# A recurrent-memory attention kernel: products of 128 weight columns made as two products of 64 side by side

## The chip, the cores and the metric

The kernel runs on one core of one Trainium2 chip. The metric is the device time of one execution in microseconds (us); lower is better. A profile is one execution taken by the hardware profiler; its span goes from the first to the last instruction.

## What is computed

Two layers of attention with a recurrent memory (A), each followed by a dense block (B), over 2048 tokens of width 512, in bf16. Attention goes by segments of 32 tokens; ahead of each segment stand 8 memory rows, which are the first 8 output rows of the segment before it, so that segments of one layer must follow one another. There are 32 heads of 128.

```python
for s in range(n_seg):                                   # 64 segments
    h = concatenate([mem, xs], axis=1)                   # 8 + 32 = 40 rows
    q, k, v = h @ Wq, h @ Wk, h @ Wv                     # 32 heads of 128
    scores = where(mask, q @ k.T * scale, -1e9)
    o = (softmax(scores) @ v) @ Wo
    mem = o[:, :M]; outs.append(o[:, M:])

x = x + A(layernorm(x)); x = x + B(layernorm(x))         # B: relu(x @ w1) @ w2, inner width 1376
x = x + A(layernorm(x)); x = x + B(layernorm(x))         # the same weights again
```

## The kernel before

All weights stay in SBUF. The work is a chain of 68 steps, written out one after the other. Step k does segment k of the first layer (act 0) and segment k - 4 of the second layer (act 1), as far as both exist: steps 4 to 63 are the 60 two-layer steps (`single` is false), the four before and the four after have one layer. The two segments of a two-layer step lie side by side in the tile `HT` (512 features in four chunks c4, by 2 x 40 rows), so that one product with the query or key weights has 80 moving columns; in a one-layer step it has 40.

In a step, in this order on TensorE:

- `qk(0, ...)`: queries and keys of heads 0 to 15, in batches of 6, 6 and 4 heads (`qk_batch`). Each head takes four accumulating products of 128 x 128 weights (`lhsT` = `W_sb`, `rhs` = `HT`), 128 products in all, into PSUM tiles `qp` of a pool of three banks. ScalarE casts the queries to `QT` (L597), VectorE the keys to `KT` (L599).
- `block`: some products of the output projection of the step before (`wox`, L373: 64 weight columns, 256 moving columns, in the left and the right half of the array's columns in turn, named by `tile_position`), in some steps also value products (`vp`, L310).
- `scores` (L625): 32 products of 40 weight columns, again left and right in turn.
- `qk(1, ...)`: queries and keys of heads 16 to 31, another 128 products. While they run, VectorE and ScalarE make the exponentials of the first half.
- `dense_h` (L522): the first dense product of segment k - 2, 11 x 4 = 44 products of 128 x 128 weights with up to 64 moving columns; ScalarE applies the relu. In the steps with value products it is cut in two parts, with other work between.
- scores of the second half, more of `block`, the second dense product (`dense_y`, L543, 64 weight columns), the transposes of the second half's probabilities (`transpose_p`, L675, 64 weight columns), the weighted values (L701), the output of the memory rows (L633), values of the next step (L354), the new memory (L857) and its values (L797).

The order on TensorE, VectorE, GpSimd and the DMA-issuing SyncE is the order written in the program (`manual_schedule` names these four); on ScalarE the order is a planner's. `tc.high_priority` marks the chain of the recurrence for that planner.

A product in the program is two instructions on TensorE, a weight load (PEld in the profile) and the product proper (PE).

Of the kernel before, what the change touches and what calls it, by code (L numbers as in the profile page):

```python
# [22 lines left out]
def kernel(  # L23
# [14 lines left out]
    nc = tc.nc  # L38
    _, S, Dm = A_x.shape
    _, H, Dh = A_Wq.shape[0], A_Wq.shape[1], A_Wq.shape[2]  # L40
# [4 lines left out]
    L = M + SEG  # L45
# [4 lines left out]
    NC4 = Dm // 128  # L50
# [45 lines left out]
    def span(d):  # L96
        offs = ([0] if has0(d) else []) + [o for o, _ in slots_of.get(d, [])]
        return base(d) + min(offs), base(d) + max(offs) + 32
# [52 lines left out]
    w1_sb = const.tile([128, NC4, Dff], BF)  # L151
# [35 lines left out]
    HT = const.tile([128, NC4, 2, L], BF)  # L187
# [95 lines left out]
    def layers(k):  # L283
        return [a for a in range(2) if (has0, has1)[a](k)]
# [216 lines left out]

    def dense_h(d, parts=slice(None), behind_exp=False):
        if not 0 <= d <= LAST:
            return
        lo, hi = span(d)
        n = hi - lo

        def cols(c4):  # L510
            return xnT_tiles[d + 2][:, c4, lo:hi]

        if not parts.start:
            hT_tiles[d] = wk.tile([128, NFC, 64], BF, tag="hT", bufs=1, name="hT")
        hT = hT_tiles[d]
        pieces = ((8, NFC), (0, 4), (4, 8)) if d == LAST - 1 else ((8, NFC), (0, 8))
        for f0, f1 in pieces[parts]:
            hp = ps_fill.tile([128, 8, 64], F32, tag="fill", name="hp")
            for fc in range(f0, f1):
                u = F_LAST + 128 * fc if fc < NFC - 1 else 0  # L520
                for c4 in range(NC4):
                    nc.tensor.matmul(hp[:, fc - f0, 0:n], lhsT=w1_sb[:, c4, u:u + 128],  # L522
                                     rhs=cols(c4), start=(c4 == 0), stop=(c4 == NC4 - 1))
            if (f0, f1) == (4, 8):
                nc.vector.tensor_scalar_max(out=hT[:, f0:f1, 0:n], in0=hp[:, 0:f1 - f0, 0:n], scalar1=0.0)
            elif behind_exp:
                with tc.issue_after(last_exp[0].ins):
                    nc.scalar.activation(out=hT[:, f0:f1, 0:n], in_=hp[:, 0:f1 - f0, 0:n], func=ACTF.Relu)
            else:
                nc.scalar.activation(out=hT[:, f0:f1, 0:n], in_=hp[:, 0:f1 - f0, 0:n], func=ACTF.Relu)  # L530
# [51 lines left out]
    def qk_batch(n, h0, nh, a_lo, a_hi, between=None):  # L582
        ncol = (a_hi - a_lo) * L
        res = {}

        for W_sb, nm in (((Wq_sb, "QT"), (Wk_sb, "KT")) if n < 2 else ((Wk_sb, "KT"), (Wq_sb, "QT"))):
            qp = ps_c.tile([128, HB, 2 * L], F32, tag="c")
            for hi in range(nh):
                h = h0 + hi
                for c4 in range(NC4):  # L590
                    nc.tensor.matmul(qp[:, hi, 0:ncol], lhsT=W_sb[:, c4, h * Dh:(h + 1) * Dh],  # L591
                                     rhs=HT[:, c4, a_lo:a_hi, :], start=(c4 == 0), stop=(c4 == NC4 - 1))
            dst = wk.tile([128, nh, 2 * L], BF, tag=f"{nm}{n}", bufs=1, name=nm)
            if nm == "QT":
                if between:
                    between()
                nc.scalar.copy(out=dst[:, 0:nh, a_lo * L:a_hi * L], in_=qp[:, 0:nh, 0:ncol])  # L597
            else:
                nc.vector.tensor_copy(out=dst[:, 0:nh, a_lo * L:a_hi * L], in_=qp[:, 0:nh, 0:ncol])  # L599
            res[nm] = dst  # L600
        return res["QT"], res["KT"]
# [3 lines left out]
    def qk(hf, act, between=None, behind=None):  # L605
        res = []
        for n, (o, nh) in enumerate(BATCHES):
            res.append((o, nh) + qk_batch(n, 16 * hf + o, nh, act[0], act[-1] + 1, None if n else between))
            if n == 0 and behind:
                behind()  # L610
            if hf and n > 0 and (n == 2 or len(act) == 1):
                masks(*act[n - 1:n])
        return res
# [319 lines left out]
    def step(k):  # L933
# [54 lines left out]
        if single:  # L988
            block(k, part, mid)
        elif light:  # L990
            dense_h(k - 2, slice(0, 1))
            block(k, part, 16)
        else:
            dense_h(k - 2)
# [3 lines left out]
        if single:  # L998
            dense_h(k - 2, slice(0, 1) if k == LAST else slice(None))
            block(k, mid, H)  # L1000
            if k == LAST:
                keep_busy(3)
        elif light:
            dense_h(k - 2, slice(1, None), True)
            block(k, 16, H)
        else:
            if not single:
                evict_behind.append(last_exp[0].ins)
            block(k, part, H)
            evict_behind.clear()  # L1010
# [56 lines left out]
    with tc.manual_schedule(engines={mybir.EngineType.PE, mybir.EngineType.DVE, mybir.EngineType.SP,  # L1067
# [23 lines left out]
        d = LAST - 1  # L1091
# [10 lines left out]
        for fc in order:  # L1102
            fs = 128 if fc < NFC - 1 else F_LAST
            for q in range(4):
                u, j = divmod(q, 2)
                nc.tensor.matmul(sp_banks[0][32 * q:32 * q + 32, 0:256], lhsT=hT_tiles[d][0:fs, fc, SEG * u:SEG * u + SEG],  # L1106
                                 rhs=w2_flat[0:fs, fc * Dm + 256 * j:fc * Dm + 256 * j + 256],
                                 start=(fc == order[0]), stop=(fc == order[-1]), tile_position=(0, 32 * q))
# [42 lines left out]
```

## Time and profile before

| | us |
|---|---|
| median of 3 runs | 1582.98 |
| lowest, highest | 1580.97, 1584.96 |
| span of the profiled execution | 1580.0 |
| TensorE busy (PE) | 1548.6, 98% |
| weight loads (PEld) | 1286.3, 81% |
| VectorE busy | 1277.3, 81% |
| ScalarE busy | 734.7, 47% |
| GpSimd busy | 349.8, 22% |

Of the profiled execution the page gives the span alone; it lies 1.0 us under the fastest run and 3.0 under the median, which is what stands before the first and behind the last instruction and the spread between runs. Busy times of TensorE contain the tail of the last product of a group, so products are better compared by the distance from one start to the next.

### The profile page before, as it was taken

To read this page: it belongs to the slowest core of one execution; us is meant where nothing else is said; L and a number is where in the kernel's file an instruction comes from. 1 tells how busy PE (TensorE), PEld (TensorE's weight loads), DVE (VectorE), ACT (ScalarE), POOL (GpSimd) and SP (SyncE) were. 2 spreads that over 40 slices of the span, in tenths; PEclk is the share of its full clock that TensorE was granted. 3 is DMA by queue.
4 is the path that set the end of the run, shared out by engine and by line. 5 is a ranking of instruction groups with operands and counts; after the bars stand their busy time and mean duration, and the time that the engine had idled before them with its cause. 6 is when DMAs were issued, how large, how long until landed. Compare 5 with 4: busy or idle time off the path is not lost. (4 is left out here: it accounts for less than half of the span.)

```text
span 1580.0 us, 95139 instructions
## 1 busy us (share of the span) xinstructions
PE 1548.6 (98%) x42866; PEld 1286.3 (81%) x42866; DVE 1277.3 (81%) x3300; ACT 734.7 (47%) x1762; POOL 349.8 (22%) x670
## 2 busy tenths in 40 slices
PE   5899999999999999999999999999999999999998
PEld 3677888888888888888888888988888898888876
DVE  3578888888888888888888888888888888887866
ACT  3435445454544545454454545445454544545433
POOL 2012122222222222222122222212222221222110
PEclk9999999999999999999999999999999999999999
DMA  9734432434353244434433343443443344333331
GB/s 369 246 77 76 87 84 78 81 92 79 78 92 84 78 82 94 80 76 91 84 80 80 99 80 76 88 84 79 77 99 77 72 87 80 82 74 95 75 69 41
DMA packets 222021, 146.26 MB, mean 93 GB/s; under 512 B 123464, under 2 KB 215984, under 8 KB 221616
## 3 DMA queue, kind: packets, MB, share of 16 engines
q1 hardware_dynamic: 218448, 135.96, 38.8%
q8 instruction: 336, 5.51, 1.5%
q0 software_dynamic: 3072, 4.20, 1.1%
q14 instruction: 69, 0.57, 0.1%
q10 hardware_dynamic: 96, 0.03, 0.0%
HBM read 65.41 MB, written 45.35 MB: 70 GB/s over the span
## 5 line engine op out<-in xcount | busy, mean ns | idle before, releaser
L597 ACT CAST QT<-qp 128x480 bf16<-128x480 f32 (+3 forms) x408 | 201.5, 494 | 433.4 <-PE qp L591 433.1
L591 PE MATMUL qp<-HT,Wq_sb 128*128 128x80 bf16 (+1 forms) x8704 | 371.3, 200 | 3.2 <-POOL HT L786 1.2
L591 PEld LDWEIGHTS <-Wq_sb 128*128 128x128 bf16 x8704 | 325.9, 100 | 35.2 <-issue 27.5
L591 PE MATMUL qp<-HT,Wk_sb 128*128 128x80 bf16 (+1 forms) x8704 | 347.3, 199 | 1.7 <-issue 1.3
L591 PEld LDWEIGHTS <-Wk_sb 128*128 128x128 bf16 x8704 | 319.5, 100 | 2.6 <-issue 1.6
L664 POOL TENSOR_TENSOR P_sb<-es,sm 128x320 bf16<-128x320 f32 x185 | 130.8, 721 | 714.8 <-ACT QT L597 299.4
L599 DVE CAST KT<-qp 128x480 bf16<-128x480 f32 (+3 forms) x408 | 220.3, 565 | 36.3 <-PE qp L591 32.9
L643 DVE TENSOR_REDUCE mx<-sp 128x8 f32<-128x320 f32 x256 | 115.1, 487 | 133.1 <-PE sp L625 130.9
L373 PE MATMUL wox<-Wo_sb,OTx 128*64 128x256 bf16 x2880 | 173.6, 273 | 0.0
L373 PEld LDWEIGHTS <-OTx 128*64 128x64 bf16 x2880 | 150.2, 110 | 2.9
L649 ACT ACTIVATE es<-es 128x320 f32<-128x320 f32 x256 | 109.5, 468 | 61.9 <-DVE es L647 61.0
L797 PE MATMUL vm<-Wv_sb,HTm 128*32 128x512 bf16 x2176 | 129.4, 379 | 1.8 <-DVE KT L599 1.0
L354 PE MATMUL v<-Wv_sb,xnT 128*32 128x512 bf16 x2048 | 128.8, 378 | 0.0
L633 PE MATMUL wo<-Wo_sb,OTm 128*32 128x512 bf16 x2144 | 128.6, 380 | 0.0
L659 DVE TENSOR_REDUCE sm<-es 128x8 f32<-128x320 f32 x256 | 117.4, 459 | 13.5 <-ACT es L649 5.0
L617 DVE CAST sp<-maskb 128x320 f32<-128x320 bf16 x256 | 118.3, 483 | 0.0
L647 DVE TENSOR_TENSOR es<-sp,mx 128x320 f32<-128x320 f32 x256 | 113.6, 482 | 1.5
L543 PE MATMUL sp<-w_sb,hT 128*64 128x256 bf16 (+4 forms) x1452 | 103.9, 276 | 0.4 <-issue 0.4
L522 PE MATMUL hp<-xnT,w_sb 128*128 128x64 bf16 (+1 forms) x2948 | 98.5, 192 | 0.9 <-issue 0.5
L801 ACT CAST VmS<-vm 128x512 bf16<-128x512 f32 x134 | 78.5, 586 | 44.4 <-PE vm L797 42.5
L222 POOL TENSOR_TENSOR mv<-mv,mhalf_t 128x1 f32<-128x1 f32 x82 | 45.8, 558 | 224.6 <-DVE mv L221 218.9
L797 PEld LDWEIGHTS <-HTm 128*32 128x32 bf16 x2176 | 54.7, 97 | 48.8 <-issue 3.1
(125 smaller groups left out, 2088.5 us busy)
## 6 DMA issues: line engine op xcount, KB each, us to landing
Vs<-vd SPq DMA_DIRECT2D x96, 256.0 KB
vd<-vst SPq DMA_DIRECT2D x181, 128.0 KB
vmd<-VmS SPq DMA_DIRECT2D x134, 128.0 KB
Vs<-vmd SPq DMA_DIRECT2D x254, 32.0 KB
Vs<-vmd SPq DMA_DIRECT2D x60, 128.0 KB
Wq_sb<-in_A_Wq_dram SPq DMA_DIRECT2D x2, 2048.0 KB
Wk_sb<-in_A_Wk_dram SPq DMA_DIRECT2D x2, 2048.0 KB
Wv_sb<-in_A_Wv_dram SPq DMA_DIRECT2D x2, 2048.0 KB
```

The costliest lines, as they stand in the source:

```text
L354: nc.tensor.matmul(vp[32 * j:32 * j + 32, :], lhsT=tokens[:, c4, :], rhs=Wv_sb[:, c4, n * 512:(n + 1) * 512], start=(c4 == 0), stop=(c4 == ...
L373: nc.tensor.matmul(out[64 * j:64 * j + nr, 0:256], lhsT=lhsT, rhs=rhs[:, 256 * j:256 * j + 256], start=start, stop=stop, tile_position=(0, ...
L591: nc.tensor.matmul(qp[:, hi, 0:ncol], lhsT=W_sb[:, c4, h * Dh:(h + 1) * Dh], rhs=HT[:, c4, a_lo:a_hi, :], start=(c4 == 0), stop=(c4 == NC4 ...
L597: nc.scalar.copy(out=dst[:, 0:nh, a_lo * L:a_hi * L], in_=qp[:, 0:nh, 0:ncol])
L599: nc.vector.tensor_copy(out=dst[:, 0:nh, a_lo * L:a_hi * L], in_=qp[:, 0:nh, 0:ncol])
L617: nc.vector.tensor_copy(out=sp_tiles[a], in_=maskb2)
L633: nc.tensor.matmul(wo[32 * j:32 * j + 32, :], lhsT=OTm[:, h, n, 2 * M * c:2 * M * c + 4 * M], rhs=Wo_sb[:, h, :], start=(h < 4), stop=(h > ...
L643: nc.vector.tensor_reduce(out=mxs[a][:], in_=sp, axis=AX.X, op=ALU.max)
L647: nc.vector.tensor_tensor(out=es[:], in0=sp, in1=mxs[a][:].unsqueeze(2).to_broadcast([128, 8, L]), op=ALU.subtract)
L659: nc.vector.tensor_reduce(out=sm[:], in_=es[:], axis=AX.X, op=ALU.add)
L664: eng.tensor_tensor(out=P, in0=es[:], in1=sm[:].unsqueeze(2).to_broadcast([128, 8, L]), op=ALU.mult)
L797: nc.tensor.matmul(vp[32 * j:32 * j + 32, :], lhsT=HTm[:, c4, :], rhs=Wv_sb[:, c4, n * 512:(n + 1) * 512], start=(c4 == 0), stop=(c4 == NC ...
```

## The change

A helper `product` takes the place of the matmul call in `qk_batch` and in `dense_h`. Where `narrow` is set it makes the product of 128 weight columns as two of 64: the left half of the weight columns into PSUM partitions 0 to 63, the right half into 64 to 127, with the same moving data and the same accumulation. It is set for the second half's queries and keys in two-layer steps (`ncol == 2 * L and h0 >= 16`) and for the first dense product of segments whose step has two layers. The results land where they did. TensorE's instruction list grows from 85,734 to 106,374 rows.

```diff
+    def product(out, lhsT, rhs, c4, narrow):
+        if not narrow:
+            nc.tensor.matmul(out, lhsT=lhsT, rhs=rhs, start=(c4 == 0), stop=(c4 == NC4 - 1))
+            return
+        for j in range(2):
+            cols = slice(64 * j, 64 * j + 64)
+            nc.tensor.matmul(out[cols], lhsT=lhsT[:, cols], rhs=rhs, start=(c4 == 0), stop=(c4 == NC4 - 1),
+                             tile_position=(0, 64 * j))
...
                 for c4 in range(NC4):
-                    nc.tensor.matmul(hp[:, fc - f0, 0:n], lhsT=w1_sb[:, c4, u:u + 128],
-                                     rhs=cols(c4), start=(c4 == 0), stop=(c4 == NC4 - 1))
+                    product(hp[:, fc - f0, 0:n], w1_sb[:, c4, u:u + 128], cols(c4), c4, len(layers(d + 2)) == 2)
...
                 for c4 in range(NC4):
-                    nc.tensor.matmul(qp[:, hi, 0:ncol], lhsT=W_sb[:, c4, h * Dh:(h + 1) * Dh],
-                                     rhs=HT[:, c4, a_lo:a_hi, :], start=(c4 == 0), stop=(c4 == NC4 - 1))
+                    product(qp[:, hi, 0:ncol], W_sb[:, c4, h * Dh:(h + 1) * Dh], HT[:, c4, a_lo:a_hi, :], c4,
+                            ncol == 2 * L and h0 >= 16)
```

## The prediction

> **What bounds the kernel now.** I read the page first, for the engine that carries the span, then the groups of instructions kept apart by shape, for what one product costs in each tile form.
>
> ```profile
> span 1580.0 us, 95139 instructions
> PE 1548.6 (98%) x42866; PEld 1286.3 (81%) x42866; DVE 1277.3 (81%) x3300; ACT 734.7 (47%) x1762; POOL 349.8 (22%) x670
> PEclk9999999999999999999999999999999999999999
> q8 instruction: 336, 5.51, 1.5%
> L591 PE MATMUL qp<-HT,Wk_sb 128*128 128x40 bf16 x1024 | 31.6, 180 | 1.0 <-issue 0.6 <-DMA Wk_sb<-in_A_Wk_dram 0.3
> L522 PE MATMUL hp<-xnT,w_sb 128*128 128x64 bf16 x2684 | 90.5, 193 | 0.4 <-DVE xnT L445 0.4
> L675 PE MATMUL tp<-ident,P_sb 128*64 128x80 bf16 x1136 | 32.8, 202 | 0.7 <-DVE P_sb L664 0.6
> L373 PEld LDWEIGHTS <-OTx 128*64 128x64 bf16 x2880 | 150.2, 110 | 2.9
> PE sp L213 <- POOL maskb L175: 4.6, 1, 4.6
> PE qp L591 <- issue: 2.5, 6, 0.6
> ```
>
> TensorE is busy for 98% of the span at the full granted clock, and in the list of waits (the last two rows, longest first) no engine holds it up: the longest is 4.6 us, once, at the start. So time is what the stream of products costs on TensorE. The span is 1580.0 us; the three runs took 1580.97 to 1584.96, median 1582.98, so what I add to the span I add to the median.
>
> The second of those waits is small but odd: six times TensorE waits for "issue", that is, for nothing that the profile shows. And the row of q8 says how instructions arrive: 336 packets, 5.51 MB. That is 16.4 KB a packet; 42,866 products and as many weight loads are 85,732 instructions, so 64 bytes each and 255 or 256 to a packet. To see whether the two belong together I looked at the timeline of one such wait, and at the windows between four waits of the kind.
>
> ```profile
> 1040.75 0.81 PE L591 MATMUL qp<-HT,Wq_sb 128*128 128x80 bf16 x18
> 1042.07 0.38 PE L591 MATMUL qp<-HT,Wq_sb 128*128 128x80 bf16 x6 [0.51 <-issue]
> 98.21 1.15 PE L591 MATMUL qp<-HT,Wk_sb 128*128 128x40 bf16 x40
> 102.10 0.36 PE L522 MATMUL hp<-xnT,w_sb 128*128 128x32 bf16 x8 [0.48 <-issue]
> 650.98:1042.07 391.10, 390.58 (x10821) 329.61 (x10821) 330.11 (x850) 186.71 (x449) 91.99 (x174) 1.00 0.41 84
> 1042.07:1388.08 346.01, 345.82 (x9548) 290.93 (x9547) 287.88 (x740) 166.85 (x401) 80.39 (x151) 1.00 0.41 82
> 1388.08:1457.76 69.68, 69.67 (x1911) 58.26 (x1911) 57.33 (x148) 34.16 (x82) 15.49 (x27) 1.00 0.37 84
> 1457.76:1480.66 22.90, 22.90 (x641) 19.52 (x637) 18.89 (x50) 10.59 (x25) 5.16 (x9) 1.00 0.36 76
> 75.74:79.82 4.08, 3.41 (x132) 3.20 (x129) 2.21 (x6) 1.13 (x3) 1.16 (x2) 1.00 0.66 106
> 94.64:98.10 3.46, 3.46 (x133) 3.18 (x131) 3.10 (x9) 1.12 (x3) 0.00 (x0) 1.00 0.44 111
> 98.10:102.10 4.00, 3.52 (x134) 3.14 (x130) 2.69 (x8) 0.90 (x3) 1.97 (x5) 1.00 0.41 97
> ```
>
> The wait at 1042.07 falls into the middle of a batch, after 18 of 24 equal products. The first four windows go from one such wait to the next; the second number in brackets counts the weight loads. Twice 10,821, 9,547, 1,911 and 637 is 21,642, 19,094, 3,822 and 1,274, which are 85, 75, 15 and 5 blocks of 256 less 118, 106, 18 and 6: in each case 1.2 to 1.4 a block, for rows of the sequencer that these columns don't count. So the waits stand at the edges of blocks of 256 instructions: TensorE has run out of instructions there. The last three windows each hold one block at such edges, in one-layer steps where products are shortest: a block came every 4.08, 3.46 and 4.00 us, mean 3.85. I take **3.85 us** as the price of a block (256 instructions, 128 products with their weight loads), 3.46 and 4.00 as its bounds. That a wait can occur at all while the mean block lasts 1580/336 = 4.7 us says that only one block is fetched ahead.
>
> The Trainium skill, "Runtime: NRT & Kernel Launch", section "Instruction fetch mechanics", describes blocks of 256 instructions, fetched while the block before runs, and calls the cost of crossing an edge mostly hidden. The trace agrees on the block and, so far, on "mostly" (2.5 us of such waits in 1580); by that rule the change would pay nothing for instructions, which is the first rival below.
>
> **One two-layer step.** The timeline of TensorE through one step; columns are start, duration of the group (with the tail of its last product), and the group.
>
> ```profile
> 711.51 1.03 PE L591 MATMUL qp<-HT,Wq_sb 128*128 128x80 bf16 x24
> ...
> 716.77 0.56 PE L625 MATMUL sp<-KT,QT 128*40 128x40 bf16 x32
> 717.26 1.03 PE L591 MATMUL qp<-HT,Wq_sb 128*128 128x80 bf16 x24
> 718.13 1.03 PE L591 MATMUL qp<-HT,Wk_sb 128*128 128x80 bf16 x24
> 718.99 1.03 PE L591 MATMUL qp<-HT,Wq_sb 128*128 128x80 bf16 x24
> 719.85 1.60 PE L591 MATMUL qp<-HT,Wk_sb 128*128 128x80 bf16 x40
> 721.28 0.74 PE L591 MATMUL qp<-HT,Wq_sb 128*128 128x80 bf16 x16
> 721.86 1.45 PE L522 MATMUL hp<-xnT,w_sb 128*128 128x64 bf16 x44
> 723.24 0.57 PE L625 MATMUL sp<-KT,QT 128*40 128x40 bf16 x32
> 723.66 3.12 PE L373 MATMUL wox<-Wo_sb,OTx 128*64 128x256 bf16 x54
> ...
> 727.62 0.45 PE L675 MATMUL tp<-ident,P_sb 128*64 128x80 bf16 x16
> 727.90 0.39 PE L543 MATMUL sp<-w_sb,hT 128*64 128x256 bf16 x4
> ...
> 734.59 0.60 PE L591 MATMUL qp<-HT,Wq_sb 128*128 128x80 bf16 x12
> ```
>
> What counts is start to start. A wide product of 80 columns costs (718.13 - 717.26)/24 = 36 ns. The step lasts 734.59 - 711.51 = 23.08 us. The 32 scores before the second half take 717.26 - 716.77 = 0.49, those after the dense products 723.66 - 723.24 = 0.42: the former end in a change from 64-column tiles to the full array, the latter do not, so that change costs about 0.08 us. The 44 dense products take 1.38 us with a change back; inside the group two of them are (1.45 - 0.193)/43 = 29 ns apart (the group's duration without the tail of its last product, 193 ns), at which 44 would take 1.28, so that change costs about 0.10.
>
> **The change, part by part.** *The array.* Each of 128 query and key products and 44 dense products of a two-layer step becomes two of 64 weight columns, in the left and right column tiles. The trace has this form exactly, with other data: the transposes of L675, 64 weight columns, 80 moving columns, tiles left and right in turn. 16 of them take 727.90 - 727.62 = 0.28 us, 35 ns a pair. So a pair costs what the wide product costs, 35 against 36: 128 pairs 4.48 us. A dense pair of 64 columns lies between 29 and 35; I take 29, the rate of the wide one. Scores, second half, dense and scores, now 6.89 us (716.77 to 723.66), would take 0.41 + 4.48 + 1.28 + 0.41 = 6.6: a gain of 0.3 us a step by the two tile changes that go, since everything in this stretch then has 64 columns. Steps with value products between have two more such changes. Over 60 steps: **-20 us**, bounds -30 and 0.
>
> *The weights.* A load of 64 columns is shown at 110 ns (L373), far longer than a pair; the 17.5 ns a product of L675, loads included, say that loads run behind the products before them. The Trainium skill, "TensorE: Matmul & The Clock Gate", section "LDWEIGHTS", gives columns/1.2 ns for a load, and "TensorEngine Tiling (Array Packing)", "Gotcha 2", says that column tiling excludes the fast weight load: an estimate by these pages is 53 ns for each half and 107 a pair that takes turns, 12 us a step and over 700 in all. L675 speaks against it; the case is the last rival.
>
> *The instructions.* The instruction lists of the two kernels have 85,734 and 106,374 rows on TensorE: 20,640 more, 344 for each of 60 steps (172 products and 172 loads). The step of before has 646 products, 1,292 instructions with their loads and some 7 of the sequencer, 5.1 blocks; that leaves 23.08/5.1 = 4.5 us a block, above 3.85. After it has 6.4 blocks. What decides is their place: in the stretch from scores to scores stand 32 + 256 + 88 + 32 = 408 products, 816 instructions, 3.2 blocks, which the array would run at 8 ns an instruction, 2.06 us a block. They arrive at 3.85.
>
> The sum for that stretch: let a share f of the running block be used up when it begins. The first half's products before it run 4.6 us a block, so the next block was asked for 4.6f us ago and is there after 3.85 - 4.6f, or when the rest of this one is used up, 2.06(1-f), whichever is later. Then come two more edges at 3.85 each (three if f is over 0.81), and the rest at 8 ns. For f = 0, 0.25, 0.5, 0.75 and 1 the stretch takes 11.9, 11.3, 10.7, 10.2 and 11.9 us, mean over f 11.0. The sequencer hands instructions over ahead of the array, so the first edge is hurt less; no row shows by how much. Bounds: nothing, and the whole excess of the first edge, about 1.1 us. I take 0.6. So 10.4 us stand against 6.89: **+3.5 us a step, +210 us over 60 steps**, the gain above included. By the same working 3.46 us a block give a mean of 9.9 and 4.00 give 11.4. With 3.46 and 1.1 of lead that is +1.9 a step, +115; with 3.46 and the lead of 0.6, +145; with 4.00 and no lead +4.5, +271. The stretches after it (products of 256 and 512 columns) are slow enough for their blocks and take none of it back: a block fetched early saves one edge, not three.
>
> *ScalarE.* Its order is not written by hand, and one thing in it moves: in two-layer steps the two exponentials of the first half now go ahead of the first query cast of the second.
>
> ```profile
> 718.39 0.56 ACT L597 CAST QT<-qp 128x480 bf16<-128x480 f32 x1 [1.66 <-PE qp L591]
> 718.85 0.83 ACT L649 ACTIVATE es<-es 128x320 f32<-128x320 f32 x2
> ```
>
> That cast would end at 718.85 + 0.83 + 0.56 = 720.24 instead of 718.95, and the second batch of keys (719.85) needs its bank, the oldest of three: 0.4 us of wait, 23 us over 60 steps, if the products came at today's pace. While TensorE waits up to 1.8 us at each edge of the same stretch it is covered; I price it at nothing. VectorE, GpSimd and the DMA queues keep their work and their order.
>
> So: 1583 + 210 = **1793 us**.
>
> **Rivals.** *Instructions keep up* (the rule of the Runtime page): faster. It needs a block within 2.06 us, or several fetched ahead. Then the 20 us of tile changes are won, 1563, less what of the 23 us of the ScalarE wait shows, 1586 at worst. For it: only 2.5 us of "issue" in the list. Against it: the windows at 3.46 to 4.08 us, in which TensorE stands still at the edge. 0.07, of which 0.05 faster and 0.02 the same.
> *Blocks are limited on average only*, with more than one in hand: 6.4 x 3.85 = 24.7 us a step, +1.6, +97: 1680. Against it: waits occur now, at a mean of 4.5 us. 0.06.
> *The halves don't overlap but take turns*, each at the pace of the shortest wide products, (1.15 - 0.180)/39 = 25 ns (98.21, with the tail of 180 ns): pairs at 50, 128 x 14 + 44 x 21 ns = 2.7 us a step, +163, 1746; with late instructions on top little more than the forecast, as 25 ns a product is 3.2 us a block, still under 3.85. 0.06.
> *Weight loads bind*: loads run beside each other but not behind products, a pair takes the 110 ns of L373's load, 74 more than now, 172 x 60 times: +764, 2347. For it: that row; against it: L675. The rule of the LDWEIGHTS section comes to nearly the same. 0.01.
>
> **How the numbers follow.** The forecast has 0.80. The range is 1728 to 1854: from the low block price with the middle lead (+145) to the high price with no lead (+271), which also holds the third rival; the first, second and last lie outside, and the low price with the long lead. Under 0.3% (about 5 us, what a measurement of this kernel can tell from no change) I call the same. Faster 0.05, same 0.02, slower 0.93.
>
> **What would show it.** Right: "issue" becomes TensorE's largest wait, some 3 times a step, 1 to 1.8 us each, in the second half's products and the dense ones; q8 near 416 packets; no two edges under 3.4 us apart; pairs at about 35 ns between edges; no gap of 0.1 us at the two tile changes. Wrong: pairs at 50 ns or more without gaps (the array or the loads), or a stretch of about 6.6 us without gaps (instructions keep up).

## The result, and the profile after

The changed kernel takes 1820.11 us in the median of 6 runs (1810.21 to 1827.8), the kernel before 1582.73 on the same chips (1580.97 to 1584.96). The ratio is 1.1504, with a 95% interval from 1.147 to 1.1537: slower by 237 us. Forecast were 1793, in a range from 1728 to 1854. The profiled run is one of the faster, 1812.67 us; the two faster runs had a mean granted clock of 0.997 and 0.998, the four slower (1815 to 1828 us) of 0.990 to 0.993, the profile of the kernel before 1.000.

The page of the changed kernel, its span, the busy times, TensorE's instruction packets and the shares of the chain that ended last; then the list of TensorE's waits (total us, times, longest):

```profile
span 1811.0 us, 115866 instructions
...
PE 1582.9 (87%) x53185; PEld 1308.5 (72%) x53186; DVE 1286.7 (71%) x3300; ACT 737.6 (41%) x1762; POOL 349.1 (19%) x670
...
q8 instruction: 417, 6.83, 1.6%
...
PE 85%; issue 11%; DMA 1%; DVE 1%; ACT 1%; SPq 1%; POOL 0%; ACTq 0%; POOLq 0%
...
PE qp L510 <- issue: 98.6, 96, 2.1
PE hp L510 <- issue: 60.7, 43, 2.3
PE sp L633 <- issue: 19.1, 13, 2.6
PE wox L373 <- issue: 11.7, 14, 1.5
...
PE wo L641 <- issue: 3.2, 5, 0.9
PE vp L310 <- issue: 2.0, 2, 1.1
...
PE qp L510 <- ACT QT L605: 1.2, 2, 1.0
```

TensorE's own work hardly grew: 1582.9 us busy, 34 more, some 31 of it the tails of 0.18 us in front of the 173 new gaps (a product lasts 202 ns and the next starts after 18). What grew is idle time, and it has one name: "issue", 173 times in the six rows above that bear it, 195 us, and 11% of the chain. Of waits for another engine the largest of the new products is 1.2 us (the ScalarE casts, last row). 417 instruction packets came instead of 336.

Where in a step: windows of the parts of a step (first half; from scores to scores; the rest), first of before, then two steps of after. The first number behind the window is its length, then come busy us and instructions of PE and of PEld (the other engines, the clock and the DMA follow).

```profile
711.50:716.77 5.27, 5.27 (x142) 5.20 (x140) 4.24 (x10) 2.30 (x5) 0.55 (x1) 1.00 0.72 198
716.77:723.66 6.89, 6.89 (x242) 6.80 (x236) 5.21 (x14) 2.82 (x7) 1.93 (x3) 1.00 0.40 44
723.66:734.59 10.93, 10.93 (x285) 7.80 (x277) 9.88 (x27) 5.64 (x15) 2.84 (x6) 1.00 0.16 39
```

```profile
704.89:710.15 5.26, 5.26 (x144) 5.19 (x141) 4.24 (x10) 2.13 (x4) 0.55 (x1) 1.00 0.83 214
710.15:719.19 9.04, 7.16 (x412) 6.93 (x408) 5.35 (x13) 2.78 (x7) 1.94 (x3) 1.00 0.25 57
719.19:731.20 12.01, 11.20 (x286) 7.90 (x279) 9.94 (x27) 5.76 (x15) 2.83 (x6) 1.00 0.05 14
731.20:736.46 5.26, 5.26 (x142) 5.19 (x140) 4.54 (x11) 2.11 (x4) 0.56 (x1) 1.00 0.87 211
736.46:746.88 10.42, 7.37 (x414) 7.04 (x408) 5.32 (x14) 2.75 (x8) 1.93 (x3) 1.00 0.58 60
746.88:757.95 11.07, 11.07 (x285) 7.95 (x277) 9.94 (x27) 5.76 (x15) 2.85 (x6) 1.00 0.06 18
```

The first half keeps its 5.26 us. The stretch from scores to scores has 408 weight loads where it had 236; it takes 9.04 and 10.42 us instead of 6.89, of which 7.16 and 7.37 are busy. The rest of the step is as before in the second of these steps (11.07) and 1.1 us longer in the first (12.01): the step whose stretch got off lightly pays behind it. Over the 44 steps without value products the starts in the trace give a mean stretch of 10.33 us (before 6.98) and a mean rest of 11.54 (before 10.95); the 16 steps with them, 9.64 (6.65) and 11.50 (10.94). Over all 60 steps the stretches grew by 196 us and the rests by 35, together all of the 231 us by which the span grew.

The timeline of the second of these stretches, and the place in the first step where it pays (start, duration, group, idle time before it and what ended it):

```profile
736.46 0.56 PE L633 MATMUL sp<-KT,QT 128*40 128x40 bf16 x32
736.87 1.03 PE L510 MATMUL qp<-HT,Wq_sb 128*64 128x80 bf16 x48
737.73 1.03 PE L510 MATMUL qp<-HT,Wk_sb 128*64 128x80 bf16 x48
...
741.75 0.48 PE L510 MATMUL qp<-HT,Wk_sb 128*64 128x80 bf16 x16 [0.80 <-issue]
742.06 0.74 PE L510 MATMUL qp<-HT,Wq_sb 128*64 128x80 bf16 x32
742.64 1.43 PE L510 MATMUL hp<-xnT,w_sb 128*64 128x64 bf16 x80
746.32 0.32 PE L510 MATMUL hp<-xnT,w_sb 128*64 128x64 bf16 x8 [2.25 <-issue]
746.47 0.56 PE L633 MATMUL sp<-KT,QT 128*40 128x40 bf16 x32
```

```profile
719.19 0.93 PE L373 MATMUL wox<-Wo_sb,OTx 128*64 128x256 bf16 x13
720.94 2.45 PE L373 MATMUL wox<-Wo_sb,OTx 128*64 128x256 bf16 x41 [0.81 <-issue]
```

Scores to halves is 736.87 - 736.46 = 0.41 us, without the 0.08 of a tile change, and 48 halves take 737.73 - 736.87 = 0.86, what 24 whole products took (0.87). So halves do run side by side. From the gap that ends at 741.75 to the one that ends at 746.32 stand 16 + 32 + 80 = 128 products, one block of 256 instructions; they were run in 2.1 us and the next came 4.57 us after the one before.

### The profile page after: what moved, and what is told of

The parts are those of the page before. It is cut to its first block, busy times and chain, and to the rows that moved or that the text cites. A ratio compares the mean times of both kernels' runs of the same rounds, so it can differ in the third digit from the quotient of the medians.

```text
span 1811.0 us, 115866 instructions
## 1 busy us (share of the span) xinstructions
PE 1582.9 (87%) x53185; PEld 1308.5 (72%) x53186; DVE 1286.7 (71%) x3300; ACT 737.6 (41%) x1762; POOL 349.1 (19%) x670
## 4 chain that ended last, share of the span: by engine, by line
PE 85%; issue 11%; DMA 1%; DVE 1%; ACT 1%; SPq 1%; POOL 0%; ACTq 0%; POOLq 0%
PE qp L506 18%; PE qp L510 16%; PE wox L373 9%; PE wo L641 7%; PE vm L805 6%; PE v L354 6%; PE hp L510 5%; PE sp L551 4%; PE pv L709 3%; PE sp L633 3%; PE vp L310 3%; DMA Wv_sb<-in_A_Wv_dram 1%; PE tp L683 1%; PE wox L396 1%; PE hp L506 0%
## 5 line engine op out<-in xcount | busy, mean ns | idle before, releaser
L510 PE MATMUL qp<-HT,Wq_sb 128*64 128x80 bf16 x7680 | 178.3, 202 | 50.8 <-issue 50.8
L510 PE MATMUL qp<-HT,Wk_sb 128*64 128x80 bf16 x7680 | 169.5, 202 | 49.7 <-issue 47.8
L506 PE MATMUL qp<-HT,Wq_sb 128*128 128x80 bf16 (+1 forms) x4864 | 201.9, 198 | 2.0 <-POOL HT L794 1.2
L506 PEld LDWEIGHTS <-Wq_sb 128*128 128x128 bf16 x4864 | 177.6, 99 | 31.5 <-issue 26.3
L510 PEld LDWEIGHTS <-Wk_sb 128*64 128x64 bf16 x7680 | 153.7, 113 | 59.1 <-issue 58.4
L510 PEld LDWEIGHTS <-Wq_sb 128*64 128x64 bf16 x7680 | 156.1, 113 | 54.3 <-issue 54.3
L506 PE MATMUL qp<-HT,Wk_sb 128*128 128x80 bf16 (+1 forms) x4864 | 189.1, 197 | 1.7 <-issue 1.0
L506 PEld LDWEIGHTS <-Wk_sb 128*128 128x128 bf16 x4864 | 173.9, 99 | 2.1 <-DMA Wk_sb<-in_A_Wk_dram 1.2
L510 PE MATMUL hp<-xnT,w_sb 128*64 128x64 bf16 (+1 forms) x5280 | 104.7, 196 | 60.7 <-issue 60.7
L510 PEld LDWEIGHTS <-w_sb 128*64 128x64 bf16 x5280 | 94.2, 113 | 63.7 <-issue 63.7
## 6 DMA issues: line engine op xcount, KB each, us to landing
vd<-vst SPq DMA_DIRECT2D x181, 128.0 KB
vmd<-VmS SPq DMA_DIRECT2D x134, 128.0 KB
Vs<-vmd SPq DMA_DIRECT2D x60, 128.0 KB
```

The costliest lines, as they stand in the source:

```text
L506: nc.tensor.matmul(out, lhsT=lhsT, rhs=rhs, start=(c4 == 0), stop=(c4 == NC4 - 1))
L510: nc.tensor.matmul(out[cols], lhsT=lhsT[:, cols], rhs=rhs, start=(c4 == 0), stop=(c4 == NC4 - 1), tile_position=(0, 64 * j))
```

## The experiments

Three theories. A, the forecast's: instructions come late, a block of 256 in about 3.8 us, one ahead. B: the halves themselves are slow, in the array or in their loads. C: each instruction costs the same wherever it stands.

**One part alone.** In e1_dense_only only the dense products are made in halves; the call for queries and keys is given `False`:

```diff
-                    product(qp[:, hi, 0:ncol], ..., ncol == 2 * L and h0 >= 16)
+                    product(qp[:, hi, 0:ncol], ..., False)
```

> Only the first dense products are made in halves; the query and key products stay whole. 5,280 more rows on TensorE than before. Theory A (instructions come late: a block of 256 takes about 3.8 us, one is fetched ahead, and the loss arises only where the array runs through a block faster): +23 to +35 us over before, since the stretch has 408 - 128 = 280 products and the wide ones in it run at 36 ns. Theory B (the halves themselves are slow on the array or in their loads): the loss goes with the number of halved products, 237 x 44/172 = +61 us. Theory C (every added instruction costs the same wherever it stands): 5,280 x 237/20,640 = +61 us.

Measured: 1604.35 us against 1581.95, ratio 1.0141 (1.0119 to 1.0163), +22.4 us. e2_qk_only is the opposite, `False` in the dense call.

> Only the second half's query and key products are made in halves; the dense products stay whole. 15,360 more rows. Theory A: +150 to +170 us, the waits in the query and key products and the scores behind them. Theories B and C: 237 x 128/172 = +176 us. By A the two parts alone come to less than the whole (237), by B and C to the whole.

Measured: 1761.13, ratio 1.1127 (1.1106 to 1.1149), +179.2 us. The waits of both, the largest rows of each, e1 first:

```profile
PE sp L633 <- issue: 6.1, 7, 1.3
...
PE qp L506 <- issue: 2.0, 7, 0.7
PE wo L641 <- issue: 1.8, 3, 0.9
PE wox L373 <- issue: 1.7, 4, 0.8
PE hp L510 <- issue: 1.6, 5, 0.6
```

```profile
PE qp L510 <- issue: 98.2, 101, 1.7
PE sp L633 <- issue: 26.7, 37, 1.7
PE wox L373 <- issue: 10.9, 12, 1.3
```

The dense part costs a third of what B and C say and a little less than A's lowest figure: its 88 halves are less than a block, and the wide products ahead of them can leave one in stock (that this is why was not tested). Only about 10 of its 22 us are waits for "issue" (13.9 in the whole list, 4.1 before); some 8 are the dense pairs themselves, 32 ns each where the whole product took 29, which A's estimate did not have. The larger part, e2, lies 9 us over A's range and would by itself suit B and C; by the starts in its trace the stretches grew by 160 us, which is within that range, and the rests by 20. The two come to 202 of 237, so parts do not add up, as A says and B and C do not.

**The same instructions without tiles.** In e3_split_moving the narrow branch of `product` cuts the moving columns instead:

```diff
+        half = out.shape[-1] // 2
+        for j in range(2):
+            moving = rhs[:, j, :] if len(rhs.shape) == 3 else rhs[:, half * j:half * j + half]
+            nc.tensor.matmul(out[:, half * j:half * j + half], lhsT=lhsT, rhs=moving, ...)
```

> The same products are cut in two along the moving columns instead (128 weight columns, 40 or 32 moving): as many instructions in the same places, no column tiles, and all tile changes of before stay. Each half costs 25 ns on the array, so that the array alone loses (50 - 36) x 7,680 + (50 - 29) x 2,640 ns = +163 us. Theory A: +225 to +245 us, with issue waits in these products as with the change. Theory B: +163 us without issue waits. Theory C: +163 and the 237 of the instructions, +400 us.

Measured: 1817.75, ratio 1.1489 (1.1466 to 1.1512), +235.8 us, in A's range.

```profile
L511 PE MATMUL qp<-HT,Wq_sb 128*128 128x40 bf16 x7680 | 229.2, 180 | 12.2 <-issue 11.7
...
L511 PE MATMUL hp<-xnT,w_sb 128*128 128x32 bf16 x5016 | 141.3, 176 | 12.2 <-issue 11.2
```

TensorE is busier here (1745.1 us against 1582.9), the waits are shorter, and the end is the same as with column tiles (1820). Two kernels whose products differ by some 155 us on the array (50 ns a pair against 36 and 32), with the same instructions in the same places, take the same time: what binds is the instructions, not the halves.

**As many instructions elsewhere.** e4_slow_place leaves the tested products whole and cuts the long ones (here, shortened, one of four places):

```diff
-                nc.tensor.matmul(vp[32 * j:32 * j + 32, :], lhsT=HTm[:, c4, :],
-                                 rhs=Wv_sb[:, c4, n * 512:(n + 1) * 512], ...)
+                    for c in range(0, 512, 256): ...
+                        nc.tensor.matmul(vp[32 * j:32 * j + 32, c:c + 256], lhsT=HTm[:, c4, :],
+                                         rhs=Wv_sb[:, c4, n * 512 + c:n * 512 + c + 256], ...)
```

> Before, with nearly as many added instructions (18,560 rows) where products are long: those of 512 moving columns (values, memory values, memory output) are cut into two of 256, those of 256 of the output projection into two of 128; the tested products stay whole. On the array about +13 us. Theory A: these stretches then come near the price of a block but not far over it, +85 to +105 us. Theory B: +13 us. Theory C: 18,560 x 11.5 ns = +213 us.

Measured: 1671.52, ratio 1.0563 (1.0541 to 1.0584), +89.6 us, in A's range and far from the others. Its waits now stand in other lines:

```profile
PE wo L639 <- issue: 16.6, 23, 1.1
PE qp L595 <- issue: 12.5, 28, 1.6
PE vm L806 <- issue: 9.0, 25, 1.6
PE v L355 <- issue: 7.7, 17, 1.0
```

90% of the rows that the change adds cost 38% of its time, because they stand where the array was slow. C falls.

**The price by itself.** e5_bursts, run once, is before with six bursts on TensorE at its end, when the DMA engines have nearly nothing left to do (4 GB/s in that part of the page). The function `burst` takes the number of products, whether they are whole, and the moving columns; its body is left out here.

```diff
+        burst(512, True, 80)
+        burst(512, False, 80)
+        burst(512, False, 160)
+        burst(512, True, 40)
+        burst(512, False, 160)
+        burst(512, False, 64)
```

> Before, with bursts of products at its end whose results nobody uses, after nearly all DMA work is done: (1) 512 whole products of 80 moving columns, (2) 512 pairs of halves of 80, (3) 512 pairs of 160, (4) 512 whole of 40, (5) 512 pairs of 160, (6) 512 pairs of 64. Theory A: (1) 18.4 us, no wait (4.6 us a block); (2) 8 blocks at 3.5 to 3.85 us, 28 to 31 us; (3) and (5) about 35 us, no wait (4.4 us a block); (4) 4 blocks, 14 to 15.4 us; (6) as (2), 28 to 31 us. Theories B (in the array) and C (a price per instruction): (2) by B whatever a pair costs there, without idle gaps at every 128th product; by C the price shows in (3) as in (2). If halves run freely, (2) is 18.4, (4) 12.8 and (6) 16.3 us.

```profile
1578.57 21.33 PE L1117 MATMUL probe<-HT,Wq_sb 128*128 128x80 bf16 x661
1600.10 2.48 PE L1117 MATMUL probe<-HT,Wq_sb 128*64 128x80 bf16 x128 [0.20 <-issue]
1603.85 2.48 PE L1117 MATMUL probe<-HT,Wq_sb 128*64 128x80 bf16 x128 [1.26 <-issue]
...
1618.55 2.48 PE L1117 MATMUL probe<-HT,Wq_sb 128*64 128x80 bf16 x128 [1.26 <-issue]
1622.02 2.85 PE L1117 MATMUL probe<-HT,Wq_sb 128*64 128x80 bf16 x128 [0.99 <-issue]
1625.49 45.11 PE L1117 MATMUL probe<-HT,Wq_sb 128*64 128x160 bf16 x1408 [0.62 <-issue]
1671.04 40.97 PE L1117 MATMUL probe<-HT,Wq_sb 128*128 128x40 bf16 x1280 [0.44 <-issue]
1712.78 2.21 PE L1117 MATMUL probe<-HT,Wq_sb 128*64 128x64 bf16 x128 [0.77 <-issue]
1716.53 2.21 PE L1117 MATMUL probe<-HT,Wq_sb 128*64 128x64 bf16 x128 [1.53 <-issue]
1720.00 2.21 PE L1117 MATMUL probe<-HT,Wq_sb 128*64 128x64 bf16 x128 [1.26 <-issue]
```

(A row can begin in one burst and end in the next.) The halves of 80 and of 64 stop at every 128th product, neither earlier nor later, and a block comes every 3.47 or 3.75 us, once after 4.02. Between the stops a half of 80 takes (2.48 - 0.20)/127 = 18 ns, 36 a pair, a half of 64 (2.21 - 0.20)/127 = 15.8, 32 a pair. The halves of 160, which need 4.5 us a block (burst (5): 35.7 us for 8 blocks), run for over 1,000 products without a stop. By the starts in the trace burst (1) took 18.5 us, as forecast, (3) 36.4, of which 0.6 are the wait of a last late block, and (5) 35.7, against about 35. Bursts (2) and (6) took 26.9 us and (4) 13.5, 0.5 to 1.1 us under A's range: a block was in stock when they began.

The instruction packets of the same stretch, from 1599 to 1623 us in slices of 0.6 us:

```profile
GB/s 0 0 0 27 0 0 0 0 0 27 0 0 0 0 0 0 27 0 0 0 0 0 27 0 0 0 0 0 27 0 0 0 0 0 27 0 0 0 0 0
...
q8 instruction: 6, 0.10, 1.7%
```

The six packets of queue 8 are all that the DMA engines move here, one to a block. The packet times in the trace say when: in all 13 intervals between two late blocks one packet starts, 1.1 to 1.5 us after the first product of the running block; it takes 0.9 to 1.4 us, and TensorE goes on 1.3 to 1.5 us after its end. So while blocks come late the next one is fetched only after the running one has begun: one block ahead, no more.

**Half of the change.** e6_late_part has `h0 >= 28` instead of `h0 >= 16`.

> Halves only for the last query and key batch of a two-layer step (32 of the 128 products) and the dense products behind it: 76 of the 172 products, 9,120 rows more. Theory A: +63 to +77 us. Theories B and C: 237 x 76/172 = +105 us.

Measured: 1659.08 against 1583.2, ratio 1.0467 (1.0439 to 1.0495), +75.9 us, in A's range.

```profile
PE hp L510 <- issue: 19.7, 29, 1.4
PE sp L633 <- issue: 15.0, 14, 1.6
PE wox L373 <- issue: 14.4, 16, 1.6
PE wo L641 <- issue: 5.7, 10, 0.9
```

Here 44% of the halves cost 32%, and a large part of the waits stands behind them, in the output products: in the 44 steps without value products the stretches grew by 37 us and the rests by 28, by the starts in the trace. No version came out that beats the kernel before: the two tile changes are worth under 0.2 us a step, and each way to save them tried here adds instructions to the stretch that has least room for them.

## Why the prediction was right, point by point

- *What bounds the kernel.* The reading that a 0.5 us wait for "issue" marks the edge of a block of 256 instructions held: e5 shows the same wait at every 128th product.
- *The price of a block*, 3.85 us with bounds 3.46 and 4.00. In e5 it is 3.47 or 3.75, once 4.02. In the changed kernel, where two waits for "issue" in a row stand 128 products apart (104 times), the starts in the trace give 3.76 us on average. Right; but the upper bound is not one, as 11 of the 104 came after 4.28 to 4.84 us. That one block is fetched ahead was a mere inference from waits at a mean of 4.7 us a block; the packets of e5 show it.
- *The stretch*, 10.4 us instead of 6.89: 10.33 in the 44 steps without value products. Right, but that it fits to 0.1 us is in part luck. The means over f were taken from five values and miss the jump at 0.81; worked out by the same rule they are 11.1 us for 3.85, 10.0 for 3.46 and 11.6 for 4.00, 0.1 to 0.15 more than written. And the lead of 0.6 us was about the middle of its bounds, with no row behind it. e5 has one: 21 halves into burst (2), at 1597.4, a block begins, and the next one is there at 1600.10, 2.7 us later and not 3.47 or 3.75 as from then on, a lead of 0.8 to 1.0 us. In the 16 other steps the stretch went from 6.65 to 9.64; the forecast counted them like the rest. Over the 60 steps the stretches cost 196 us, not 210.
- *What comes behind the stretch takes none of it.* This step failed. The rest of a step grew by 0.6 us: 26 us over the 44 steps without value products and 9 over the 16 with them, where a part of the dense halves stands in the rest. The forecast fell short by 27 us (1793 against 1820), in the profiled run by 21 (231 us more span against 210): 35 too few here and 14 too many in the stretches partly cancel. The stretch ends inside a block that was entered late, and the next edge falls into the output products, which then wait as at 720.94. The rows wox, wo and vp of the list of waits have 16.9 us of it, in 21 waits, to which the tails of the products in front of them add.
- *The array's gain*, -20 us. The tile changes went, as said. The pair of 80 costs 36 ns and not 35, the dense pair 32 and not 29: in 2,640 pairs 8 us, and 128 x 60 pairs at 1 ns another 8. So the gain was at most a few us of the forecast's 20. The bound of 35 ns a dense pair was there; I took the other end.
- *ScalarE's new order*, priced at nothing: 1.2 us in the list of waits. Right here.
- *Packets*, 416 forecast, 417 came; *waits*, some 3 a step: 173 over 60. Their size, forecast at 1 to 1.8 us, goes from 0.2 to 2.6, with a median of 1.1.
- *Rivals.* "Instructions keep up": no, issue is 11% of the chain. The rule of the Trainium skill, "Runtime: NRT & Kernel Launch", section "Instruction fetch mechanics", that crossing an edge is mostly hidden, holds in e5 for whole products of 80 columns (4.6 us a block) and for halves of 160 (4.5), and not at 2.0 to 2.3 us a block. "Limited on average only": no, 1820 is above 1680, and a block in hand didn't help beyond one edge. "Halves take turns" and "weight loads bind": no, 36 ns a pair with its loads.

The 9 us by which e2 lies over A's range are again the step that failed, as its rests grew by 20 us. What stays open is e1: its stretches grew by 14 us, of which some 8 are the dense pairs on the array, and its rests by 10; why its stretches wait so much less than A's lowest figure is not shown.

## What to carry to other kernels

Before cutting products into smaller ones, count instructions: on TensorE a product and its weight load are two, a block of 256 arrives here every 3.5 to 4 us with one in stock, so that a run of more than about 128 products needs some 27 to 31 ns each (tested down to 16 ns on the array). The price is set by the place: 20,640 more instructions cost 237 us in a fast stretch, 18,560 cost 90 in slow ones. What a stretch leaves unpaid can fall due behind it, in products that by themselves are slow enough. In a profile the sign is a short idle time that ends by "issue", in the middle of a run of equal products; count the weight loads between two of them.

## What the runs showed of the hardware that was not expected

- A late block comes at steps of about 0.27 us: in e5 3.47, 3.75 or once 4.02 us after the one before (to 0.02), in the changed kernel, in all 104 cases, 3.45 to 3.48, 3.73 to 3.76, 4.00 to 4.02, 4.28, 4.57 or 4.84. In e5 the packets themselves took 0.88 to 0.99 us in the intervals of 3.47 and 1.15 to 1.45 in the longer ones, but for one of 0.92 that started 0.3 us later than the rest. What makes the steps is not shown. The mean is 3.64 us in e5, where instructions are all the traffic (4 GB/s), and 3.76 in the changed kernel, at a mean of 82 GB/s.
- The clock was not full throughout. In the profile of the changed kernel the granted clock is 0.50 for two stretches of 3.4 us, at 128.0 and 1606.0 us, the first from within an "issue" wait of 1.55 us on, the second 0.4 us after one of 1.98 us; that the waits bring it about is not shown. The 54 output products at 1606.27 take 4.65 us, against 3.12 at 723.66 in the profile before. A mean clock of 0.990, the lowest of the six runs, is by the same measure some 11 such stretches (an estimate: 0.01 x 1826 / (0.5 x 3.4)). The forecast has no term for it.
- Halves of 64 moving columns cost 32 ns a pair, whole products of 64 columns 29, while at 80 columns both cost 36. Why the pair costs more at 64 is not shown.
